# A fused sigmoid attention and MLP: from batch 2 on TensorE takes its work in the order of the program

## The chip, the cores and the metric

The kernel runs on one core of a Trainium2 chip. The metric is the device time of one execution in microseconds (us); lower is better. A core has five engines with a queue of instructions each: TensorE (PE, matmuls; its weight loads are listed apart as PEld), VectorE (DVE), ScalarE (ACT), GpSimd (POOL) and SyncE (SP, which here issues most transfers). An engine takes its queue in order, and an instruction waits there until semaphores tell that its operands are ready and its destination is free.

## The reference

```python
scores = scale * np.matmul(q, k.transpose(0, 1, 3, 2)) - np.log(S)
attn = 1.0 / (1.0 + np.exp(-scores))
x = np.matmul(attn, v)              # batch 8, heads 12, S = 448, D = 64; heads side by side: 3584 x 768
h = x @ w_in                        # 768 x 2048
g = np.where(h >= 1, h, np.where(h <= -1, 0.0, (h + 1) ** 2 / 4))
out = g @ w_out                     # 2048 x 768
```

All inputs and the output are float32.

## The kernel before

Numbers are split into a high and a low float16 part, and a product is three float16 matmuls (high x high, high x low, low x high). The first batches are prepared together with the weights; from batch 2 on the work of a batch is always the same (batch 7 has no attention beside it), and in it lies the change.

**Attention** works ahead: while batch b goes through the MLP, the attention of batch b + 1 is computed. Heads go in six pairs, and a pair is cut into four pieces of keys: three full ones (128 keys of both heads) and a middle one (64 keys of each head). `scores` writes a piece's scores to a PSUM tile `psc`, of which there are two: L416 and L411 with the whole array, L425 with two matmuls that use half of the array's rows each. L159 is one small matmul that sums a pair's magnitudes. `weigh` turns a piece into weights: sigmoid L457 (ScalarE, in place in `psc`), a cast to the high part L465 (ScalarE), the low part L466 (VectorE). `av` multiplies them with v, L498, in matmuls that use half of the array's columns and come in pairs. At a pair's end L507 copies the result out; L131 to L139, L359 and L360 (VectorE) make the scales of a later pair, and L344 (ScalarE) takes its magnitudes. GpSimd splits the raw q, k and v into parts (L378 to L380).

**The up product** (x @ w_in) goes in eight blocks i = 0 to 7. A block has seven products j = 0 to 6 of half size, written (i,j) here; each is a unit of nine matmuls of 224 columns (L688). The products are summed in quarters of two PSUM tiles `ph`: (i,0), (i,1) and (i,4) in the first, (i,2), (i,3), (i,5) and (i,6) in the second. Between them the kernel reads the tiles: L700 (ScalarE) and one L697 (VectorE) after (i,1), two L697 after (i,3), L706 (ScalarE) after (i,4), two L697 after (i,6). Then `bend` makes g: Relu L735 (ScalarE), L736 and L737 (VectorE), the cast L738 (ScalarE) and the low part L739 (VectorE), twice per block. The units' order is (0,0) to (0,3), and then, for each i, (i+1,0), (i+1,1), (i,4), (i,5), (i,6), (i+1,2), (i+1,3). L664 loads the weights of a block, three blocks ahead at most. **The down product** (g @ w_out) goes in 48 units of six matmuls of 448 columns (L758), eight to each of six output tiles `po`; L768 scales one, and it is stored. `ph` and `po` share three PSUM tiles.

**The order of the work.** For each batch the program has a list of units, 56 up and 48 down, and calls `step` between them at even distances until the next batch's attention is done, 12 unit places before the end. A step that does work writes the scores of two pieces and, behind them, `av` of the two pieces of the step before. There are 12 in a batch, called S0 to S11 here: S0 stands before (0,0), S1 to S7 lie in the up stage, some 7.7 units apart; even ones score a full and a middle piece, odd ones two full pieces.

What the program writes is not yet the order in which an engine takes it. A scheduler orders each engine's instructions by priority and a model of their times: where the next one of the program would not be ready in the model, it takes another. Only inside `manual_schedule` does an engine keep the order in which the program wrote its instructions. The loop over batches has this for TensorE, from batch `PM` on:

```python
            if b >= PM:
                order.enter_context(tc.manual_schedule(engines={mybir.EngineType.PE}))
```

With `PM = 9` and eight batches it is never entered.

Of the kernel before, what the change touches and what calls it, by code (L numbers as in the profile page):

```python
# [14 lines left out]
F32 = mybir.dt.float32  # L15
# [3 lines left out]
AF = mybir.ActivationFunctionType  # L19
ALU = mybir.AluOpType  # L20
# [3 lines left out]
P = 128  # L24
# [12 lines left out]
NA = 8  # L37
# [9 lines left out]
GPOOL = 1  # L47
POOL_FROM = 6
WI_SUM = 2
WO_SUM = 0  # L50
MAX_ACT = 47
L0 = 9
A0 = 19
# [2 lines left out]
SB = 2  # L56
# [4 lines left out]
MIXP = 0  # L61
CORN = 10
TP = 1

DW = 8
MIX0 = 8
MIX1 = 85
Q_PRIO = 72

PM = 9  # L70
WI_PRIO = 280
X_PRIO = 593

# [2 lines left out]
def sigmoid_attention_mlp(ctx: ExitStack, tc: tile.TileContext, first_qvk, qkv, w_in, w_out, out_t):  # L76
    nc = tc.nc
    NFULL, _, _, S = first_qvk.shape
    B = out_t.shape[1] // S
    NFC, _, DM = w_out.shape  # L80
# [6 lines left out]
    GROUPS = slice(0, NA), slice(NA, NFC)  # L87
# [7 lines left out]
    out_p = ctx.enter_context(tc.tile_pool(name="outp", bufs=2))  # L95
# [4 lines left out]
    ps_mo = ctx.enter_context(tc.tile_pool(name="ps_mo", bufs=3, space=PSUM))  # L100
# [24 lines left out]
    def scales(m, n, tag, pool=None, square=False, less=0):  # L125
# [24 lines left out]
        out=ident, in_=ident, pattern=[[-1, P]], compare_op=ALU.is_equal, fill=0.0, base=0, channel_multiplier=1  # L150
# [28 lines left out]
    class Weight:  # L179


        def __init__(self, dram, sb, name, spare):
            self.dram, self.sb, self.name, self.spare = dram.bitcast(I32), sb, name, spare
            self.words, self.at, self.loaded = {}, 0, 0
            self.scale, self.inv = [], []
            self.most = const.tile([P, 2, NFC], F32, name=name + "_most")
            nc.vector.memset(self.most, 0.0)
            mod = WI_SUM if name == "wi" else WO_SUM
            self.summed = [f for f in range(NFC) if mod and f % mod == 0 and f not in (NA - 1, NFC - 1)]

        def f32(self, f):
            return self.sb[:, f + 1].rearrange("p h n -> p (h n)").bitcast(F32)
# [16 lines left out]

        def convert(self):  # L210

            f = self.at - 2
            if 0 <= f < NFC:
                w = self.words.pop(f)
                if f in self.summed:

                    dump = wo.f32(-1) if self is wi else w[:, :DM].bitcast(F32)
                    nc.scalar.activation(dump, self.f32(f), AF.Abs, accum_out=self.most[:, 1, f : f + 1])
                if self is wo:
                    self.load(3 if f == 3 else 1)  # L220
            f = self.at
            if f < NFC:
                a = self.f32(f)
                nc.scalar.activation(a, self.words_of(f)[1].bitcast(F32), AF.Abs)
                if f in self.summed:
                    (nc.vector if f >= CLAMP else nc.gpsimd).tensor_scalar(
                        out=a, in0=a, scalar1=HIGH_MIN, scalar2=None, op0=ALU.max
                    )
            f = self.at - 1
            if 0 <= f < NFC:  # L230
# [395 lines left out]
    def mix(i):  # L626
# [87 lines left out]
    hold = {}  # L714
# [28 lines left out]
    def down(b, m, u, k):  # L743

        lo, hi = (0, NFC) if k is None else (GROUPS[k].start, GROUPS[k].stop)
        if u == 0:
            hold["po"] = ps_mo.tile([P, 512], F32, tag="mo", name="po")
            hold["o"] = out_p.tile([P, S], F32, tag="o", name="o")
            if m == 0:
                hold["od"] = down_sc[b, k]()  # L750
            if k == 1:
                nc.sync.dma_start(out=hold["o"], in_=part[m])
        po, o = hold["po"], hold["o"]

        pair = (u, u + NFC // 2) if b >= SB else (lo + 2 * u, lo + 2 * u + 1)
        for f in pair:
# [210 lines left out]
```

## Time and profile before

| | |
|---|---|
| time, median of 3 runs | 1190.35 us (1187.74 to 1190.66) |
| profiled execution: time, span | 1187.38 us, 1185.7 us |
| granted TensorE clock, mean | 0.991 |
| PE busy | 1144.9 us, 97% |
| DVE busy | 854.9 us, 72% |
| ACT busy | 697.6 us, 59% |
| POOL busy | 332.8 us, 28% |
| batch 3 on TensorE | from 529.17 us to 666.35 us |

An engine's share is an average over the span. A line of a group gives the source line, the engine, the operation, what it writes and reads, the count, then the busy time, the mean of one in ns, the idle time just before its instructions and what ended it. A line of a timeline gives the start, the length, the engine, the source line and the count of like instructions that follow each other.

### The profile page before, as it was taken

How to read it: one execution, taken by the hardware profiler on the slowest of the kernel's cores; microseconds unless marked ns; L12 is line 12 of the kernel's file. 1: busy time of each engine (PE TensorE's matmuls, PEld its weight loads, DVE VectorE, ACT ScalarE, POOL GpSimd, SP SyncE). 2: the span in 40 equal slices, each digit the busy share in tenths (PEclk: the TensorE clock that was granted, in tenths of full speed). 3: DMA queues.
4: the chain of work that ended last, by engine and by line, in shares of the span. 5: the costliest groups of instructions: out<-in, count | busy, mean ns of one | idle time of the engine just before them, and what ended most of it. 6: DMA issues, size and time to landing. Idle time of an engine off the chain costs nothing.

```text
span 1185.7 us, 20268 instructions
## 1 busy us (share of the span) xinstructions
PE 1144.9 (97%) x7662; PEld 669.3 (56%) x7662; DVE 854.9 (72%) x1828; ACT 697.6 (59%) x1158; POOL 332.8 (28%) x393
## 2 busy tenths in 40 slices
PE   5889899999999999999999999999999999999998
PEld 1224333444445776457754677557764577558954
DVE  6999999999956588457973689456884678736830
ACT  5886576665654577547864578455864476613510
POOL 3004410011323244234345235332532353310000
PEclk9899999999999999999999999999999999999999
DMA  9842354437542266224643065423552246302400
GB/s 367 322 153 76 118 161 152 134 119 257 182 148 72 95 217 210 76 72 142 238 163 102 30 236 208 135 64 128 204 211 64 65 147 220 126 24 87 163 16 32
DMA packets 58113, 170.01 MB, mean 143 GB/s; under 512 B 8608, under 2 KB 39840, under 8 KB 51872
## 3 DMA queue, kind: packets, MB, share of 16 engines
q1 hardware_dynamic: 56288, 159.29, 39.1%
q10 hardware_dynamic: 1728, 9.44, 2.2%
q8 instruction: 60, 0.98, 0.3%
q14 instruction: 37, 0.30, 0.1%
HBM read 126.94 MB, written 23.40 MB: 127 GB/s over the span
## 4 chain that ended last, share of the span: by engine, by line
PE 71%; DVE 17%; DMA 4%; ACT 3%; issue 2%; POOL 2%; SPq 0%; POOLq 0%; ACTq 0%; DVEq 0%
PE po L758 33%; PE ph L688 22%; PE pav L498 8%; PE psc L416 3%; PE psc L425 2%; PE ph L722 2%; DVE g L736 2%; PE psc L411 1%; DVE g L737 1%; DVE ghl L739 1%; DMA raw<-qkv 1%; DVE ahl L466 1%; DVE w_in_sb L244 1%; DVE mixa L632 1%; DVE w_out_sb L247 1%
## 5 line engine op out<-in xcount | busy, mean ns | idle before, releaser
L758 PE MATMUL po<-ghl,w_out_sb 128*128 128x448 f16 x2304 | 446.3, 353 | 1.5 <-DVE qkv_e L131 0.6
L758 PEld LDWEIGHTS <-w_out_sb 128*128 128x128 f16 x2304 | 221.7, 98 | 219.4 <-issue 15.9
L688 PE MATMUL ph<-w_in_sb 128*128 128x224 f16 x3024 | 307.7, 259 | 1.3 <-DVE g L737 0.9
L688 PEld LDWEIGHTS <-w_in_sb 128*128 128x128 f16 x3024 | 282.6, 98 | 30.1 <-issue 27.2
L466 DVE SCALAR_TENSOR_TENSOR ahl<-psc,ahl 128x896 f16<-128x896 f32 (+1 forms) x170 | 153.0, 900 | 105.7 <-ACT ahl L465 103.6
L378 POOL TENSOR_SCALAR raw<-raw,qkv_s 128x448 f32<-128x448 f32 (+1 forms) x93 | 71.0, 777 | 449.9 <-DVE qkv_i L139 346.3
L457 ACT ACTIVATE psc<-psc,nls,sqk 128x896 f32<-128x896 f32 (+1 forms) x136 | 129.5, 971 | 103.5 <-PE psc L425 86.6
L465 ACT ACTIVATE ahl<-psc 128x896 f16<-128x896 f32 (+1 forms) x170 | 126.9, 762 | 29.8 <-DVE ahl L466 28.6
L722 PE MATMUL ph<-xhl,w_in_sb 128*128 128x448 f16 x576 | 114.5, 356 | 4.7 <-DVE g L737 3.4
L344 ACT ACTIVATE dump<-raw 128x448 f16<-128x448 f32 (+1 forms) x105 | 61.9, 589 | 85.8 <-DMA raw<-qkv 84.5
L697 DVE TENSOR_TENSOR xhl<-ph,xhl 128x224 f32<-128x224 f32 x240 | 87.7, 383 | 25.3 <-PE ph L688 19.4
L738 ACT ACTIVATE ghl<-g 128x448 f16<-128x448 f32 x128 | 72.5, 573 | 44.2 <-DVE g L737 43.8
L498 PE MATMUL pav<-ahl,v 128*64 128x448 f16 x748 | 95.6, 360 | 0.0
L735 ACT ACTIVATE g<-xhl,hr,ihr 128x448 f32<-128x448 f32 x96 | 68.7, 752 | 41.9 <-DVE xhl L697 41.0
L722 PEld LDWEIGHTS <-w_in_sb 128*128 128x128 f16 x576 | 55.7, 99 | 63.6 <-issue 14.4
L736 DVE SCALAR_TENSOR_TENSOR g<-g,rk 128x448 f32<-128x448 f32 x112 | 81.4, 741 | 10.2 <-ACT g L735 10.0
L739 DVE TENSOR_TENSOR ghl<-g,ghl 128x448 f16<-128x448 f32 x128 | 85.0, 672 | 5.3 <-ACT ghl L738 4.8
L768 DVE TENSOR_SCALAR o<-po,od 128x448 f32<-128x448 f32 x48 | 32.5, 679 | 61.1 <-PE po L758 60.8
L380 POOL TENSOR_TENSOR hl<-raw,hl 128x448 f16<-128x448 f32 x62 | 71.1, 1167 | 0.0
L416 PE MATMUL psc<-qk 128*128 128x448 f16 x252 | 66.3, 354 | 2.0 <-ACT a L454 1.0
L737 DVE SCALAR_TENSOR_TENSOR g<-xhl,ihs,g 128x448 f32<-128x448 f32 x96 | 66.3, 708 | 0.3
L498 PEld LDWEIGHTS <-v 128*64 128x64 f16 x748 | 36.3, 109 | 37.9 <-issue 23.0
(167 smaller groups left out, 1198.5 us busy)
## 6 DMA issues: line engine op xcount, KB each, us to landing
w_in_sb<-blocks SPq DMA_DIRECT2D x48, 1344.0 KB, 6.1
raw<-qkv SPq DMA_DIRECT2D x34, 704.0 KB, 4.7
qk<-hl SPq DMA_DIRECT2D x320, 56.0 KB, 2.0
w_out_sb<-w_in SPq DMA_DIRECT2D x16, 768.0 KB, 8.5
out_t<-o SPq DMA_DIRECT2D x48, 224.0 KB, 1.9
blocks<-mixs SPq DMA_DIRECT2D x8, 768.0 KB, 3.5
w_out_sb<-w_out ACTq DMA_DIRECT2D x6, 768.0 KB, 4.1
raww<-w_out ACTq DMA_DIRECT2D x6, 768.0 KB, 5.7
```

The source lines that it names most:

```text
L416: nc.tensor.matmul(out, kq[:, j, 1, w], kq[:, j, 0, :], start=True, stop=False)
L457: nc.scalar.activation(a, a, AF.Sigmoid, bias=nls, scale=sqk)
L465: nc.scalar.activation(hi, x, AF.Copy, scale=ATT)
L466: nc.vector.scalar_tensor_tensor(out=lo, in0=x, scalar=ATT, in1=hi, op0=ALU.mult, op1=ALU.subtract)
L498: nc.tensor.matmul(pav[j * D : (j + 1) * D, :S], *terms[j][t], start=c == 0 and t == 0, stop=mid and t == len(terms[j]) - 1,)
L688: nc.tensor.matmul(out, w[:, wt, wh, c * P : (c + 1) * P], xc[:, xt, c, xh, :], start=j in (0, 2) and c + wh + xh == 0, stop=c == HC - 1 a ...
L697: add = lambda out, q, other: nc.vector.tensor_tensor(out=out, in0=quarter(q), in1=other, op=ALU.add)
L722: nc.tensor.matmul(ph[:, :S], w_in_sb[:, f, wh, c * P : (c + 1) * P], xhl[:, c, xh, :], start=c == 0 and wh + xh == 0, stop=c == NCC - 1 a ...
L736: nc.vector.scalar_tensor_tensor(out=g, in0=g, scalar=rt, in1=g, op0=ALU.min, op1=ALU.mult)
L737: nc.vector.scalar_tensor_tensor(out=g, in0=h, scalar=ihs, in1=g, op0=ALU.mult, op1=ALU.max)
L739: (nc.gpsimd if f % GPOOL else nc.vector).tensor_tensor(out=ghl[:, f, 1, :], in0=g, in1=hi, op=ALU.subtract)
L758: nc.tensor.matmul(po[:, :S], w_out_sb[:, f, wh, m * P : (m + 1) * P], ghl[:, f, gh, :], start=f == lo and wh + gh == 0, stop=f == hi - 1 ...
```

## The change

`PM` becomes 2: for batches 2 to 7 TensorE's instructions stand in the order of the program. Batches 0 and 1 are not touched, nor is any instruction added or removed. The scheduler still orders the other engines by its model, and since in the model TensorE now reaches its instructions at other times, the orders on VectorE, ScalarE and SyncE change with it. GpSimd's stays.

```diff
-PM = 9
+PM = 2
```

The rest of the diff leaves the work as it was: an accumulation in `convert` is written a few lines earlier in the same call, the tiles of `down` are kept under the name of their output tile, and new parameters (`SLAG`, `AM`, `MIXA`, `CUT`) stand at values that give the code of before.

```diff
-            hold["po"] = ps_mo.tile([P, 512], F32, tag="mo", name="po")
+            hold["po", m] = ps_mo.tile([P, 512], F32, tag="mo", name="po")
...
+        order = [(m, u) for m in range(NCC) for u in range(n // 2)]
+        if b >= SB:
+
+            first = [(m, u) for m in range(2) for u in range(CUT)] + [(m, u) for m in range(2) for u in range(CUT, n // 2)]
+            order[: n] = first
...
-    with tc.manual_schedule(engines={mybir.EngineType.SP}):
+    with tc.manual_schedule(engines={mybir.EngineType.SP} | ({mybir.EngineType.Activation} if AM else set())):
```

The added lines shift the numbers: a line of 131 to 139 in the kernel before is 3 higher in the changed one, one of 344 to 507 is 4 higher, one of 664 to 770 is 7 higher. The numbers in the names of tiles count tiles and differ a little between the two.

**TensorE, batch 3, step S5.** Before, after the first full piece's L416 (tile `psc_5969`) one of its two L425 is followed by products of block 4 and 5:

```order
L416 MATMUL psc_5969<-qk_5670 128x448
L425 LDWEIGHTS hl_5659
L425 MATMUL psc_5969<-hl_5659 128x448
L688 LDWEIGHTS w_in_sb_89
L688 MATMUL ph_5860<-w_in_sb_89 128x224
```

Now both pieces (`psc_5974`, `psc_5977`) are scored in one run, and `av` follows:

```order
L429 MATMUL psc_5974<-hl_5664 128x448
L429 LDWEIGHTS hl_5664
L429 MATMUL psc_5977<-hl_5664 128x448
L429 LDWEIGHTS hl_5664
L429 MATMUL psc_5977<-hl_5664 128x448
L502 LDWEIGHTS v_5359
L502 MATMUL pav_5830<-ahl_5821,v_5359 64x448
```

What moved is the products: they stand behind the whole step. Before, the step's second piece was scored five units later.

**VectorE, batch 3, from the additions after (1,6) to the two after (2,3)** (tiles `ph_5442` and `ph_5564` before, `ph_5447` and `ph_5569` now; the low parts L466 of S2's middle piece come in halves). Before:

```order
L697 TENSOR_TENSOR xhl_92<-ph_5442,xhl_92 128x224 x2
L466 SCALAR_TENSOR_TENSOR ahl_5523<-psc_5509,ahl_5523 64x448
L131 TENSOR_SCALAR qkv_e_5649<-psc_5509 128x3
L736 SCALAR_TENSOR_TENSOR g_5552<-g_5552,rk1_5145 128x448
L133 TENSOR_SCALAR qkv_e_5649<-qkv_e_5649 128x3
L697 TENSOR_TENSOR xhl_92<-ph_5564,xhl_92 128x224
L736 SCALAR_TENSOR_TENSOR g_5558<-g_5558,rk0_5135 128x448
L737 SCALAR_TENSOR_TENSOR g_5552<-xhl_92,ihs1_5149,g_5552 128x448
L135 TENSOR_SCALAR qkv_s_5652<-qkv_e_5649 128x3
L139 TENSOR_SCALAR qkv_i_5654<-qkv_e_5649 128x3
L697 TENSOR_TENSOR xhl_92<-ph_5564,xhl_92 128x224
```

Now:

```order
L704 TENSOR_TENSOR xhl_92<-ph_5447,xhl_92 128x224 x2
L470 SCALAR_TENSOR_TENSOR ahl_5524<-psc_5511,ahl_5524 128x896
L470 SCALAR_TENSOR_TENSOR ahl_5528<-psc_5514,ahl_5528 64x448
L743 SCALAR_TENSOR_TENSOR g_5557<-g_5557,rk1_5147 128x448
L704 TENSOR_TENSOR xhl_92<-ph_5569,xhl_92 128x224
L743 SCALAR_TENSOR_TENSOR g_5563<-g_5563,rk0_5137 128x448
L744 SCALAR_TENSOR_TENSOR g_5557<-xhl_92,ihs1_5151,g_5557 128x448
L470 SCALAR_TENSOR_TENSOR ahl_5528<-psc_5514,ahl_5528 64x448
L134 TENSOR_SCALAR qkv_e_5654<-psc_5514 128x3
L704 TENSOR_TENSOR xhl_92<-ph_5569,xhl_92 128x224
```

The low part of a whole piece and one more half piece have come between the two pairs of additions.

**ScalarE, batch 3, from the first sigmoid of S5 to the copy L706 after (5,4)** (tile `ph_5860` before, `ph_5865` now). Before:

```order
L457 ACTIVATE psc_5969<-psc_5969,nls_87,sqk_5656 128x2x448
L465 ACTIVATE ahl_5980<-psc_5969 128x896
L738 ACTIVATE ghl_93<-g_5795 128x448
L457 ACTIVATE psc_5972<-psc_5972,nls_87,sqk_5656 128x2x448
L735 ACTIVATE g_5911<-xhl_92,hr1_5153,ihr1_5151 128x448
L507 ACTIVATE x32_91<-pav_5825,sqk_5350 128x448
L735 ACTIVATE g_5917<-xhl_92,hr0_5143,ihr0_5141 128x448
L344 ACTIVATE dump_5965,m3_5964<-raw_5801 128x448
L465 ACTIVATE ahl_5984<-psc_5972 128x896
L706 ACTIVATE xhl_92<-ph_5860 128x224
```

Now, behind the two Relu of block 4 and one L348:

```order
L461 ACTIVATE psc_5974<-psc_5974,nls_87,sqk_5661 128x2x448
L461 ACTIVATE psc_5977<-psc_5977,nls_87,sqk_5661 128x2x448
L348 ACTIVATE dump_5970,m3_5969<-raw_5806 128x448
L745 ACTIVATE ghl_93<-g_5916 128x448
L511 ACTIVATE x32_91<-pav_5830,sqk_5355 128x448
L469 ACTIVATE ahl_5985<-psc_5974 128x896
L745 ACTIVATE ghl_93<-g_5922 128x448
L469 ACTIVATE ahl_5989<-psc_5977 128x896
L348 ACTIVATE dump_5970,m3_5969<-raw_5806 128x512
L707 ACTIVATE xhl_92<-ph_6017 128x224
L713 ACTIVATE xhl_92<-ph_5865 128x224
```

Both sigmoids now come first, and the copy that frees the product tile has moved behind both casts, two magnitudes and the copy of the next block.

More of the change, by code (lines that the diff above doesn't have):

```diff
@@ L49 @@
 WI_SUM = 2
-WO_SUM = 0
 MAX_ACT = 47
@@ L63 @@
 TP = 1
+SLAG = 2
+AM = 0
+MIXA = 0
+CUT = 8
 DW = 8
@@ L187, in __init__ @@
             nc.vector.memset(self.most, 0.0)
-            mod = WI_SUM if name == "wi" else WO_SUM
-            self.summed = [f for f in range(NFC) if mod and f % mod == 0 and f not in (NA - 1, NFC - 1)]
+            mod = WI_SUM if name == "wi" else 0
+            early = [f for g in GROUPS for f in range(g.start, g.stop - SLAG + 1)]
+            self.summed = [f for f in early if mod and f % mod == 0]
         def f32(self, f):
@@ L210, in convert @@
         def convert(self):
+            f = self.at - SLAG
+            if 0 <= f < NFC and f in self.summed:
+                nc.scalar.activation(wo.f32(-1), self.f32(f), AF.Abs, accum_out=self.most[:, 1, f : f + 1])
             f = self.at - 2
             if 0 <= f < NFC:
[L214 to L218, printed above, removed]
+                self.words.pop(f)
                 if self is wo:
@@ L654, in mix @@
             for h in range(2):
-                nc.vector.tensor_scalar(
-                    out=pv[:, h, t0 : t0 + n, :], in0=src[:, h], scalar1=to[k], scalar2=None, op0=ALU.mult
-                )
+                if MIXA:
+                    nc.scalar.activation(pv[:, h, t0 : t0 + n, :], src[:, h], AF.Copy, scale=to[k])
+                else:
+                    nc.vector.tensor_scalar(
+                        out=pv[:, h, t0 : t0 + n, :], in0=src[:, h], scalar1=to[k], scalar2=None, op0=ALU.mult
+                    )
         nc.sync.dma_start(out=blocks[i][:, : 3 * DM], in_=pl)
@@ L746, in down @@
         if u == 0:
-            hold["po"] = ps_mo.tile([P, 512], F32, tag="mo", name="po")
-            hold["o"] = out_p.tile([P, S], F32, tag="o", name="o")
+            hold["po", m] = ps_mo.tile([P, 512], F32, tag="mo", name="po")
+            hold["o", m] = out_p.tile([P, S], F32, tag="o", name="o")
             if m == 0:
@@ L751, in down @@
             if k == 1:
-                nc.sync.dma_start(out=hold["o"], in_=part[m])
-        po, o = hold["po"], hold["o"]
+                nc.sync.dma_start(out=hold["o", m], in_=part[m])
+        po, o = hold["po", m], hold["o", m]
         pair = (u, u + NFC // 2) if b >= SB else (lo + 2 * u, lo + 2 * u + 1)
@@ L788, in downs @@
         n = NFC if k is None else GROUPS[k].stop - GROUPS[k].start
-        return [lambda m=m, u=u: down(b, m, u, k) for m in range(NCC) for u in range(n // 2)]
+        order = [(m, u) for m in range(NCC) for u in range(n // 2)]
+        if b >= SB:
+            first = [(m, u) for m in range(2) for u in range(CUT)] + [(m, u) for m in range(2) for u in range(CUT, n // 2)]
+            order[: n] = first
+        return [lambda m=m, u=u: down(b, m, u, k) for m, u in order]
     def step(i):
```

## The prediction

> **What bounds the kernel now.** I read the page's busy shares and groups first, then the stretches by batch, then TensorE's timeline through one batch, then VectorE's and ScalarE's in the same batch.
>
> ```profile
> PE 1144.9 (97%) x7662; PEld 669.3 (56%) x7662; DVE 854.9 (72%) x1828; ACT 697.6 (59%) x1158; POOL 332.8 (28%) x393
> ...
> L758 PE MATMUL po<-ghl,w_out_sb 128*128 128x448 f16 x2304 | 446.3, 353 | 1.5 <-DVE qkv_e L131 0.6
> L688 PE MATMUL ph<-w_in_sb 128*128 128x224 f16 x3024 | 307.7, 259 | 1.3 <-DVE g L737 0.9
> ...
> L736 DVE SCALAR_TENSOR_TENSOR g<-g,rk 128x448 f32<-128x448 f32 x112 | 81.4, 741 | 10.2 <-ACT g L735 10.0
> ...
> w_in_sb<-blocks SPq DMA_DIRECT2D x48, 1344.0 KB, 6.1
> ```
>
> ```profile
> 545.00:605.00 60.00, 60.00 (x530) 45.51 (x528) 54.01 (x112) 47.58 (x88) 27.46 (x31) 1.00 0.63 220
> ```
>
> TensorE (PE) is the bound: 97% busy, and its two largest groups waited 1.5 and 1.3 us in all. So there is next to no idle time to win. But busy is not the same as streaming well, and the stretch from 545 to 605 (columns after the length: PE, weight loads, DVE, ACT, POOL) shows a second engine close behind: VectorE is busy 54.0 of 60.0 us in the up stage of batch 3.
>
> ```profile
> 529.17 0.54 PE L416 MATMUL psc<-qk 128*128 128x448 f16 x2
> ...
> 531.88 6.21 PE L688 MATMUL ph<-w_in_sb 128*128 128x224 f16 x63
> 537.92 0.54 PE L416 MATMUL psc<-qk 128*128 128x448 f16 x2
> 538.40 0.36 PE L425 MATMUL psc<-hl 64*128 64x448 f16 x2
> 538.69 0.55 PE L416 MATMUL psc<-qk 128*128 128x448 f16 x2
> ...
> 540.54 4.49 PE L688 MATMUL ph<-w_in_sb 128*128 128x224 f16 x45
> ...
> 572.38 0.36 PE L425 MATMUL psc<-hl 64*128 64x448 f16 x1
> 572.67 1.90 PE L688 MATMUL ph<-w_in_sb 128*128 128x224 f16 x18
> ...
> 599.71 3.76 PE L758 MATMUL po<-ghl,w_out_sb 128*128 128x448 f16 x19
> ...
> 603.31 1.89 PE L688 MATMUL ph<-w_in_sb 128*128 128x224 f16 x18
> ...
> 605.03 2.25 PE L758 MATMUL po<-ghl,w_out_sb 128*128 128x448 f16 x11
> ...
> 619.03 0.92 PE L416 MATMUL psc<-qk 128*128 128x448 f16 x4
> ...
> 621.43 8.12 PE L758 MATMUL po<-ghl,w_out_sb 128*128 128x448 f16 x42
> ...
> 629.39 0.54 PE L416 MATMUL psc<-qk 128*128 128x448 f16 x2
> ...
> 632.09 9.25 PE L758 MATMUL po<-ghl,w_out_sb 128*128 128x448 f16 x48
> ```
>
> Starts are what to read here, since ends are modelled: 63 L688 take 6.04 us (531.88 to 537.92), 0.096 each; 19 L758 take 3.60, 0.19 each. A pair of L425 halves takes 0.29 (538.40 to 538.69) and a lone half the same 0.29 (572.38 to 572.67): halves in one array run together, and each change between whole array, row halves and column halves adds about 0.1.
>
> **The gain.** In the down stage the order is already the program's, and a step stands whole there: 2.40 us with two full pieces (619.03 to 621.43), 2.70 with a middle piece (629.39 to 632.09). In the up stage the scheduler has cut the steps up. Batch 3's up stage runs from 529.17 to 605.03 and holds 3.60 us of L758 that program order puts later: 72.26 us of its own. Whole, it is S0 2.71, four steps of 2.40, three of 2.70 and 504 L688 at 6.04 per 63, 48.32: 68.7. So 3.5 us per batch of pure streaming goes, and the down stage, the same before and after, gives nothing.
>
> **The price.** Program order stops TensorE wherever the next matmul is not ready; the filler (L758 x19 at 599.71 above all) is what stood there before. I looked for such places by the waits that the order implies: a block's sixth product (i,5) overwrites the bank that both additions L697 after (i,3) read; a new PSUM tile for products waits for the last reader of the tile three back; a new score tile for L466 of the one two back. Prices are start to start, from these rows.
>
> ```profile
> 543.27 0.68 DVE L697 TENSOR_TENSOR xhl<-ph,xhl 128x224 f32<-128x224 f32 x2
> ...
> 543.86 1.08 DVE L466 SCALAR_TENSOR_TENSOR ahl<-psc,ahl 128x896 f16<-128x896 f32 x1
> 544.86 0.38 DVE L697 TENSOR_TENSOR xhl<-ph,xhl 128x224 f32<-128x224 f32 x1
> ...
> 545.16 1.27 DVE L736 SCALAR_TENSOR_TENSOR g<-g,rk 128x448 f32<-128x448 f32 x2
> ...
> 546.35 0.39 DVE L697 TENSOR_TENSOR xhl<-ph,xhl 128x224 f32<-128x224 f32 x1
> ...
> 546.65 1.27 DVE L737 SCALAR_TENSOR_TENSOR g<-xhl,ihs,g 128x448 f32<-128x448 f32 x2
> ...
> 574.40 0.63 DVE L466 SCALAR_TENSOR_TENSOR ahl<-psc,ahl 64x448 f16<-64x448 f32 x1
> 575.04 0.16 DVE L131 TENSOR_SCALAR qkv_e<-psc 128x3 f32<-128x3 f32 x1
> ```
>
> ```profile
> 538.12 0.36 ACT L706 ACTIVATE xhl<-ph 128x224 f32<-128x224 f32 x1 [0.51 <-PE ph L688]
> ...
> 538.80 2.06 ACT L457 ACTIVATE psc<-psc,nls,sqk 128x896 f32<-128x896 f32 x2 [0.32 <-PE psc L425]
> ...
> 540.78 0.92 ACT L465 ACTIVATE ahl<-psc 128x896 f16<-128x896 f32 x1
> 541.58 0.65 ACT L507 ACTIVATE x<-pav,sqk 128x448 f32<-128x448 f32 x1
> ...
> 542.10 0.93 ACT L465 ACTIVATE ahl<-psc 128x896 f16<-128x896 f32 x1
> ...
> 596.07 1.40 ACT L735 ACTIVATE g<-xhl,hr,ihr 128x448 f32<-128x448 f32 x2
> ...
> 597.38 0.56 ACT L344 ACTIVATE dump<-raw 128x448 f16<-128x448 f32 x1
> ...
> 600.79 0.57 ACT L738 ACTIVATE ghl<-g 128x448 f16<-128x448 f32 x1
> 601.26 0.62 ACT L344 ACTIVATE dump<-raw 128x512 f16<-128x512 f32 x1
> ...
> 601.87 0.35 ACT L706 ACTIVATE xhl<-ph 128x224 f32<-128x224 f32 x1
> 602.11 0.57 ACT L738 ACTIVATE ghl<-g 128x448 f16<-128x448 f32 x1
> ```
>
> A product reaches ScalarE 0.20 after its slot (537.92 to 538.12). DVE: two L697 0.59, one 0.30, L466 1.00 or 0.64 (half), L736 and L737 0.60. ACT: two L735 1.31, L344 0.56 or 0.61, two L457 1.98, L465 0.80, L507 0.52, L738 0.47, L700/L706 0.24.
>
> *A, (1,5).* Its second addition ended at 546.74. In the new order S1's first score tile is done 0.38 later (two more L416 ahead), so 547.12. TensorE, with S1 at 2.40 instead of 2.62 (537.92 to 540.54), reaches (1,5) after seven units, at 546.36. Wait 0.7.
>
> *B, (2,5).* After (1,6) VectorE's queue is the one shown with the change: 0.20 + 0.59 + 1.00 + 0.64 + 0.60 + 0.30 + 0.60 + 0.60 + 0.64 + 0.16 + 0.39 = 5.7. TensorE asks after five units, 45 L688, 4.3. Wait 1.4. Behind it stand (2,6) and S3, for whose results the Relu of block 2 and the sigmoids wait.
>
> *C, S4's middle piece.* It needs L466 of S3's second tile. From (2,6): 0.2, about 0.5 that VectorE is behind after B, 0.45 for the addition and its hand-over, then ScalarE's queue 1.31 + 0.56 + 1.98 + 0.52 + 0.56 + 0.47 + 0.80 + 0.47 + 0.93 = 7.6, and 0.35 + 1.08 to the end of L466: 10.2. TensorE asks after S3, seven units and two L416: 2.40 + 6.04 + 0.38 = 8.8. Wait 1.4.
>
> *D, (6,2).* It needs L706 of block 5, which now stands last in ScalarE's queue shown with the change. From (4,6): 0.9 to the first Relu, then 1.31 + 0.56 + 1.98 + 0.56 + 0.47 + 0.52 + 0.80 + 0.47 + 0.80 + 0.61 + 0.24 + 0.36 = 8.7: 9.6. TensorE asks after 0.86 + 2.40 + 5.18 = 8.4. Wait 1.2.
>
> Together 4.7 us per batch; the ends are 0, if every chain is ready in time, and 7.5, if two more places like C open (the rivals). I take the sum, since each place is priced by rows of its own engine. The durations are those of quiet stretches: L736 is 0.64 here and 0.74 in its group's mean, so I add 0.3 for the longer ones: 5.0, against 3.5 gained. Batches 2 to 6 do this: 5 x 1.5 = +7.5. The waits that were there, 2.8 in the two groups, are of another order; I take half as gone, -1.4. Batch 7, which has no attention left, and the first two batches, whose order stands, count nothing. SP's queue changes in one thing per batch: a weight load moves ahead of six qk loads, and at 6.1 us to landing, with more than nine units and a step (over 10 us) between issue and use, I cost that at nothing; if the queue held it 4 us longer, it would show on (i,0). POOL's order is the same.
>
> Sum: +6.1 on the profiled execution's 1187.38, which is 1193.5; the median of the runs lies 3.0 above that execution, so **1196**.
>
> The Trainium skill (TensorE: Matmul & The Clock Gate, Why this matters for your kernels) says that an idle gap beyond about 3 us puts TensorE back to half its clock. By that rule the waits above, at most 1.4, change nothing; the stretch 545 to 605 has its clock at 1.00, but also no gap, so no row here tests it.
>
> **Rivals.**
> *The gain stays (faster).* The four waits are differences of numbers near 6 to 10 us: half a microsecond less in each chain, because VectorE enters the stage earlier or ScalarE's queue is not full, leaves 2.5 of 5.0. For it: VectorE and ScalarE were idle 6.0 and 12.4 us in the 60, partly waiting on TensorE. Against: VectorE's 54.0 us of work there must now go beside 60 - 3.6 - 3.5 = 52.9 us of TensorE's. Time: 1190.35 - 5 x 1.0 - 1.4 = 1184; with no wait left at all 1190.35 - 17.5 - 2.8 = 1170. It decides at 3.0 us of waits per batch.
> *Gain and waits cancel.* Waits of 3.0 to 4.5 per batch: 1187 to 1194.
> *Waits run into each other.* A late L466 holds the next scores, these the next sigmoids: two more waits of the size of C in S5 and S7 add 2.8 per batch, 1196 + 14 = 1210. Against: between S4 and S5 and between S6 and S7 more units stand than between S3 and S4.
> *A wait passes 3 us.* By rows, a half-speed stretch of 18 L688 would cost 1.7 more after it, 5 x (3 + 1.7) = 24: 1214. This is the outcome that the clock rule above would add.
> That the change does nothing is excluded: the orders differ.
>
> **How the numbers follow.** About 0.3% (3.6 us) is what a measurement of this kernel tells from no change. Forecast, slower by 4 to 16 us: 0.45. Gain stays: 0.27. Cancel: 0.21. Waits run into each other 0.05, clock 0.02. So faster 0.27, same 0.21, slower 0.52. The forecast's own range is 1194 to 1206; to hold 8 in 10 the range takes in the faster case down to half its spread, 1178, and goes up to 1207.
>
> **What would show it.** Right: in the up stages every step is one run of L416, L425 and L498 on TensorE, S1 about 2.40; TensorE's idle time grows to some 25 us, put down to L697 (places A and B), L466 (C) and L706 (D), in batches 2 to 6 alike; the down stages keep their 61 us. Wrong: idle time under 15 us (then the chains are shorter than summed), waits ended by DMA, or a down stage that changes, which I hold for fixed.

## The result, and the profile after

| | before | after |
|---|---|---|
| time, median | 1189.05 us (4 runs, 1187.06 to 1190.66) | 1204.38 us (4 runs, 1201.26 to 1208.53) |
| ratio, 95% interval | | 1.0115 (1.0090 to 1.0141) |
| profiled execution: time, span | 1187.38 us, 1185.7 us | 1203.64 us, 1201.9 us |
| granted TensorE clock, mean | 0.991 | 0.986 |

Slower by 15.3 us; the forecast was 6 us slower than the median of then. One execution of e4 and one of e10 ran at a lower granted clock (0.75 and 0.94; 1456.48 and 1216.30 us), and the medians given below leave them out. The page of the changed kernel, busy shares and costliest groups:

```profile
PE 1134.1 (94%) x7662; PEld 672.8 (56%) x7662; DVE 867.9 (72%) x1828; ACT 696.8 (58%) x1158; POOL 337.0 (28%) x393
...
L765 PE MATMUL po<-ghl,w_out_sb 128*128 128x448 f16 x2304 | 444.7, 353 | 1.0 <-DVE qkv_e L134 0.6
...
L695 PE MATMUL ph<-w_in_sb 128*128 128x224 f16 x3024 | 301.2, 260 | 20.9 <-DVE xhl L704 15.6
...
L743 DVE SCALAR_TENSOR_TENSOR g<-g,rk 128x448 f32<-128x448 f32 x112 | 89.6, 815 | 10.9 <-ACT g L742 10.2
```

TensorE is busy for 10.8 us less, and the span is 16.2 us longer: idle time grew by 27. The products (L695) wait 20.9 us where they waited 1.3. The waits of TensorE in the whole execution (us in total, times, longest):

```profile
PE ph L695 <- DVE xhl L704: 15.6, 12, 3.7
...
PE psc L415 <- DVE ahl L470: 5.8, 6, 1.1
PE ph L695 <- ACT xhl L713: 5.2, 4, 1.3
...
PE psc L420 <- DVE ahl L470: 1.1, 5, 0.2
```

TensorE's timeline through the up stage of batch 3; the idle time ahead of a row and what ended it stand in brackets:

```profile
534.31 0.54 PE L420 MATMUL psc<-qk 128*128 128x448 f16 x2
...
543.06 0.92 PE L420 MATMUL psc<-qk 128*128 128x448 f16 x4
...
545.46 6.27 PE L695 MATMUL ph<-w_in_sb 128*128 128x224 f16 x63
552.29 1.02 PE L695 MATMUL ph<-w_in_sb 128*128 128x224 f16 x9 [0.56 <-DVE xhl L704]
...
555.85 5.35 PE L695 MATMUL ph<-w_in_sb 128*128 128x224 f16 x54
562.78 1.89 PE L695 MATMUL ph<-w_in_sb 128*128 128x224 f16 x18 [1.57 <-DVE xhl L704]
...
566.90 6.21 PE L695 MATMUL ph<-w_in_sb 128*128 128x224 f16 x63
573.33 0.55 PE L420 MATMUL psc<-qk 128*128 128x448 f16 x2 [0.22 <-DVE ahl L470]
574.95 0.73 PE L415 MATMUL psc<-hl,w_in_sb 128*128 128x448 f16 x3 [1.07 <-DVE ahl L470]
...
586.59 5.35 PE L695 MATMUL ph<-w_in_sb 128*128 128x224 f16 x54
593.25 1.88 PE L695 MATMUL ph<-w_in_sb 128*128 128x224 f16 x18 [1.31 <-ACT xhl L713]
...
608.72 5.84 PE L765 MATMUL po<-ghl,w_out_sb 128*128 128x448 f16 x30
...
673.65 0.54 PE L420 MATMUL psc<-qk 128*128 128x448 f16 x2
```

Counted in units of nine from the step ahead of them, the four stops are (1,5), (2,5), S4 and (6,2): the places A to D, in order. Now the same two executions by batch, from one (0,0) on TensorE's timeline to the next:

| stretch | before | after | difference | forecast |
|---|---|---|---|---|
| start to (0,0) of batch 2 | 394.45 | 397.80 | +3.35 | 0 |
| batches 2, 3, 4, 5 | 137.43, 137.18, 137.26, 137.93 | 139.21, 139.35, 139.20, 139.20 | +1.78, +2.17, +1.94, +1.27 | 4 x 1.5 |
| batch 6 | 133.68 | 139.12 | +5.44 | 1.5 |
| batch 7 to the end | 107.78 | 108.03 | +0.25 | 0 |

Up to the second score tile of S1 in batch 2 every engine has the same instructions in the same order in both kernels, so the first row is no effect of the order. In the profiles of this study whose text is the same up to there (e4's, at its lower clock, apart), (0,0) of batch 2 came between 393.6 and 400.2 us, with either order.

Batch 6 stands out. TensorE, VectorE and then the clock there (TensorE and VectorE as timelines, the clock as a window, its value the one before the last two columns):

```profile
995.03 4.49 PE L695 MATMUL ph<-w_in_sb 128*128 128x224 f16 x45
1003.23 4.15 PE L695 MATMUL ph<-w_in_sb 128*128 128x224 f16 x27 [3.71 <-DVE xhl L704]
```

```profile
993.15 0.38 DVE L704 TENSOR_TENSOR xhl<-ph,xhl 128x224 f32<-128x224 f32 x1
996.14 1.68 DVE L350 TENSOR_REDUCE m<-raw 128x2 f32<-128x896 f32 x2 [2.62 <-DMA raw<-qkv]
997.74 1.27 DVE L743 SCALAR_TENSOR_TENSOR g<-g,rk 128x448 f32<-128x448 f32 x2
...
1002.79 0.38 DVE L704 TENSOR_TENSOR xhl<-ph,xhl 128x224 f32<-128x224 f32 x1
```

```profile
1003.20:1008.00 4.80, 4.77 (x30) 3.74 (x30) 3.92 (x13) 1.41 (x2) 2.51 (x4) 0.64 0.32 89
```

The last pair's magnitudes are taken on VectorE (L350), not on ScalarE like the others. VectorE stood 2.62 us before them for their load, with the Relu's work and the additions L704 after (4,3) queued behind; TensorE stood 3.71 us at (4,5), and then ran at clock 0.64. The 27 L695 after the wait take 3.94 us instead of 2.59 (27 x 0.096). Before, the same instruction stood for the same load (the instructions of L346, what their engine waited for):

```profile
L346 DVE TENSOR_REDUCE m<-raw x2: 676/881/1086, 985.5 to 986.5; 128x2 f32<-128x896 f32 x1, 128x1 f32<-128x512 f32 x1
...
  DMA raw<-qkv: 2.7, 1
```

But there the scheduler had put other matmuls on TensorE, which waited 0.4 us in that stretch.

### The profile page after: what moved, and what is told of

It is laid out like the page before. It is cut to its first block, busy times and chain, and to the rows that moved or that the text cites. A ratio compares the mean times of both kernels' runs of the same rounds, so it can differ in the third digit from the quotient of the medians.

```text
span 1201.9 us, 20263 instructions
## 1 busy us (share of the span) xinstructions
PE 1134.1 (94%) x7662; PEld 672.8 (56%) x7662; DVE 867.9 (72%) x1828; ACT 696.8 (58%) x1158; POOL 337.0 (28%) x393
## 4 chain that ended last, share of the span: by engine, by line
PE 60%; DVE 27%; ACT 6%; DMA 3%; issue 3%; POOL 1%; SPq 0%; POOLq 0%; DVEq 0%; ACTq 0%
PE po L765 33%; PE ph L695 13%; PE pav L502 6%; DVE ahl L470 4%; DVE g L743 3%; PE psc L420 3%; DVE g L744 2%; DVE ghl L746 2%; DVE xhl L704 2%; PE psc L429 2%; PE psc L415 2%; ACT psc L461 1%; PE ph L729 1%; DVE mixa L636 1%; DMA blocks<-mixs 1%
## 5 line engine op out<-in xcount | busy, mean ns | idle before, releaser
L765 PE MATMUL po<-ghl,w_out_sb 128*128 128x448 f16 x2304 | 444.7, 353 | 1.0 <-DVE qkv_e L134 0.6
L765 PEld LDWEIGHTS <-w_out_sb 128*128 128x128 f16 x2304 | 221.8, 98 | 219.5 <-issue 14.3
L695 PE MATMUL ph<-w_in_sb 128*128 128x224 f16 x3024 | 301.2, 260 | 20.9 <-DVE xhl L704 15.6
L695 PEld LDWEIGHTS <-w_in_sb 128*128 128x128 f16 x3024 | 287.4, 98 | 38.8 <-issue 37.8
L470 DVE SCALAR_TENSOR_TENSOR ahl<-psc,ahl 128x896 f16<-128x896 f32 (+1 forms) x170 | 152.8, 899 | 122.1 <-ACT ahl L469 120.2
L348 ACT ACTIVATE dump<-raw 128x448 f16<-128x448 f32 (+1 forms) x105 | 61.9, 590 | 77.0 <-DMA raw<-qkv 75.6
L704 DVE TENSOR_TENSOR xhl<-ph,xhl 128x224 f32<-128x224 f32 x240 | 87.1, 382 | 22.6 <-PE ph L695 18.4
L743 DVE SCALAR_TENSOR_TENSOR g<-g,rk 128x448 f32<-128x448 f32 x112 | 89.6, 815 | 10.9 <-ACT g L742 10.2
L729 PEld LDWEIGHTS <-w_in_sb 128*128 128x128 f16 x576 | 55.6, 98 | 64.4 <-issue 15.2
L746 DVE TENSOR_TENSOR ghl<-g,ghl 128x448 f16<-128x448 f32 x128 | 86.2, 676 | 4.7 <-ACT ghl L745 3.8
L502 PE MATMUL pav<-ahl,v 128*64 128x448 f16 x748 | 84.5, 357 | 0.0
L744 DVE SCALAR_TENSOR_TENSOR g<-xhl,ihs,g 128x448 f32<-128x448 f32 x96 | 70.3, 754 | 0.0
L384 POOL TENSOR_TENSOR hl<-raw,hl 128x448 f16<-128x448 f32 x62 | 68.8, 1132 | 0.0
L420 PE MATMUL psc<-qk 128*128 128x448 f16 x252 | 63.3, 355 | 3.6 <-DVE ahl L470 1.1
L411 PE MATMUL psc<-ghl 64*128 64x448 f32 (+1 forms) x128 | 38.1, 681 | 18.6 <-ACT a L458 14.2
```

The costliest lines, as they stand in the source:

```text
L420: nc.tensor.matmul(out, kq[:, j, 1, w], kq[:, j, 0, :], start=True, stop=False)
L470: nc.vector.scalar_tensor_tensor(out=lo, in0=x, scalar=ATT, in1=hi, op0=ALU.mult, op1=ALU.subtract)
L502: nc.tensor.matmul(pav[j * D : (j + 1) * D, :S], *terms[j][t], start=c == 0 and t == 0, stop=mid and t == len(terms[j]) - 1,)
L695: nc.tensor.matmul(out, w[:, wt, wh, c * P : (c + 1) * P], xc[:, xt, c, xh, :], start=j in (0, 2) and c + wh + xh == 0, stop=c == HC - 1 a ...
L704: add = lambda out, q, other: nc.vector.tensor_tensor(out=out, in0=quarter(q), in1=other, op=ALU.add)
L729: nc.tensor.matmul(ph[:, :S], w_in_sb[:, f, wh, c * P : (c + 1) * P], xhl[:, c, xh, :], start=c == 0 and wh + xh == 0, stop=c == NCC - 1 a ...
```

## The experiments

Theory: program order saves some 3.5 us per batch in streaming, and its price is the waits at A to D, plus the load in batch 6. Rivals: the loss lies outside batches 2 to 6; whole steps save nothing; the waits are not tied to their places, since VectorE and ScalarE are simply full. Ratios are against the kernel before, with their 95% intervals.

**e1, batch 7 alone.**

```diff
-PM = 2
+PM = 7
```

> Program order on TensorE in batch 7 alone, which has no attention beside its products. Theory (the loss sits in the up stages of batches 2 to 6): within 2 us of the kernel before, so 1187 to 1191, with one wait of about 1.3 us in batch 7 (as at 1141.87 in the changed kernel). Rival (the 3.4 us by which the changed kernel was already late at the start of batch 2, where its order is the old one, or something in batch 7, belongs to the change): 1192 or more.

1189.84 us, ratio 0.9999 (0.9983 to 1.0015). Batch 7 waits 1.26 us at its last (7,5) and the time is unchanged. The first rival falls.

**e2, batches 6 and 7.**

```diff
-PM = 2
+PM = 6
```

> Program order on TensorE in batches 6 and 7 alone. Theory: batch 6 has a price of its own, since VectorE stands 2.6 us before L350 for a load of raw q, k and v, and in program order TensorE then has nothing else to take: a wait of 3.7 us and a slow stretch after it, so 133.7 us from (0,0) to (0,0) become 139.1 and the time is 1189 + 5.4 = 1194 to 1195. Rival (each batch of program order costs the same, a fifth of the 15): 1192, with no wait above 2 us.

1198.50 us, ratio 1.0074 (1.0051 to 1.0097). TensorE in batch 6:

```profile
998.03 5.20 PE L695 MATMUL ph<-w_in_sb 128*128 128x224 f16 x27 [3.59 <-DVE xhl L704]
```

The wait is there, and the 27 products behind it take 4.99 us. Batch 6 is 140.2 us, 6.5 more than before. So batch 6 has a price of its own, larger than both expectations; of the 8.6 us in the medians, 2 are not accounted for.

**e3, the last magnitudes on ScalarE.**

```diff
-MAX_ACT = 47
+MAX_ACT = 48
```

> The changed kernel (program order from batch 2), with the last pair's magnitudes on ScalarE like all others instead of L350 on VectorE. Theory: VectorE no longer stands before the load, so the 3.7 us wait at (5,5) of batch 6 goes, the wait at (6,2) of 1.3 us that the other batches have comes in its place, and the granted clock stays at 1.00 there: batch 6 falls from 139.1 to 136.5 us and the time from 1204.4 to about 1201.5. Rival (the load is what TensorE waits for, whichever engine reads it): ScalarE stands before it instead, and the time stays at 1204.

1198.22 us, ratio 1.0066 (1.0045 to 1.0087). (The wait that the expectation places at (5,5) is the one at (4,5).) Batch 6 on TensorE:

```profile
994.36 7.07 PE L695 MATMUL ph<-w_in_sb 128*128 128x224 f16 x72
...
1003.68 5.35 PE L695 MATMUL ph<-w_in_sb 128*128 128x224 f16 x54
1010.33 1.89 PE L695 MATMUL ph<-w_in_sb 128*128 128x224 f16 x18 [1.30 <-ACT xhl L713]
```

No wait at (4,5), no slow stretch, and D as in the other batches: batch 6 takes 135.0 us in place of 139.1. Batches 2 to 5 are unchanged at 139.2. The gain in the medians, 6.2 us, is more than batch 6's 4.1.

**e7, the same edit in the old order.**

```diff
-PM = 2
+PM = 9
-MAX_ACT = 47
+MAX_ACT = 48
```

> The order of before, with the last pair's magnitudes on ScalarE instead of L350 on VectorE: the control for the same edit under program order, which went from 1204.4 to 1198.2. Theory (in the old order the scheduler's filler covers the 2.7 us for which VectorE stands before the load, all but 0.4): no change, 1188.5 to 1190.5. Rival (the edit saves time by itself): 1185 or less.

1189.19 us, ratio 0.9980 (0.9964 to 0.9996): a gain, if any, of 0.2%. In the profile batch 6 takes 132.9 us instead of 133.7. What cost batch 6 4.1 us in program order cost it 0.8 in the scheduler's.

**e6, the steps one unit earlier.** The places move, the amount of work does not:

```diff
-... (at - first) < share[min(u + 1, last)] * NPIECE:
+... (at - first) < share[min(u + 0, last)] * NPIECE:
```

> The changed kernel with each step written one unit earlier among the products. Theory (the price is the four places, each a difference between two chains of 6 to 10 us, so it moves with the places): (2,5) now comes after the low part in VectorE's queue and S4 stands elsewhere, so B and C go; what stays is about 0.5 at (1,5), 1.1 at (4,2) and 1.1 at (6,2), 2.8 us in a batch in place of 4.7, and a batch takes 137 us in place of 139.2: 1194 to 1197. Rival (VectorE is full in the up stage, so that the waits only change place): 4.5 to 5 us of waits as before, 1202 to 1206.

1191.55 us, ratio 0.9996 (0.9981 to 1.0012). The stops in batch 3:

```profile
551.83 1.89 PE L695 MATMUL ph<-w_in_sb 128*128 128x224 f16 x18 [0.29 <-DVE xhl L704]
...
572.15 1.02 PE L695 MATMUL ph<-w_in_sb 128*128 128x224 f16 x9 [1.24 <-ACT xhl L713]
...
591.21 2.75 PE L695 MATMUL ph<-w_in_sb 128*128 128x224 f16 x27 [1.69 <-ACT xhl L713]
```

B and C are gone and A is halved; D, the last, is 1.69, and a stop of 1.24 at (4,2) is new. The expectation had these places, with 1.1 for each of the last two. 3.2 us of idle time remain of 4.7. A batch takes 137.4 us, as in the old order, and in batch 6 no stop is longer than 1.04 us. The time lies below the range of the theory, 1194 to 1197. One unit in the place of the steps is worth all that the change had cost (ratio 0.9996 for 1.0115); the waits belong to places. That VectorE is full whatever the place does not fit.

**e4 and e5, program order within a step alone.** The gain without the price, if they can be had apart:

```diff
-PM = 2
+PM = 9
...
-                    step(at)
+                    with ExitStack() as whole:
+                        if b >= 2:
+                            whole.enter_context(tc.manual_schedule(engines={mybir.EngineType.PE}))
+                        step(at)
```

> The kernel before, except that TensorE keeps the program's order within a step alone: the products are free to move between steps and into them. The up stage of batch 3 then changes its array layout 41 times, as often as the changed kernel, instead of 63 times, and no half matmul stands alone. Theory (whole steps save some 3.5 us per batch, and the price of the changed kernel is the waits of the products): most of the gain without most of the price, 1182 to 1187, with less than 3 us of waits in an up stage. If no wait were left, 1172. Rival (whole steps save nothing, and the saving of the changed kernel is only the idle time subtracted): 1189.

1201.26 us, ratio 1.0091 (1.0069 to 1.0114): a miss. (The expectation's 41 and 63 changes of layout fit batch 3 as a whole, where the traces have 42 and 64 from one (0,0) to the next; the up stage alone has 28 in the changed kernel and 49 in the one before.) For its profile the kernel was run again.

> The same kernel as in the run before it with program order within a step alone, for a profile at full clock; the time is known to be near 1201. Theory 1 (the freed products meet waits that an estimate of them left out, some of them long enough to cost clock): TensorE's waits in the up stages of batches 2 to 6 sum to more than 4 us per batch, and a batch takes about 139.5 us. Theory 2 (a step in one piece is not cheaper in streaming): waits below 2 us per batch, the batch still 139 us or more. Theory 3 (the loss is ahead of batch 2): batches of 136 us.

1200.24 us, ratio 1.0065 (1.0045 to 1.0085). The profiled execution, 1193.26 us, was the shortest of eight, so what follows explains less than the median lost. TensorE in batch 3, and the clock behind the first two stops:

```profile
566.59 0.55 PE L420 MATMUL psc<-qk 128*128 128x448 f16 x2 [0.74 <-DVE ahl L470]
568.69 4.60 PE L695 MATMUL ph<-w_in_sb 128*128 128x224 f16 x29 [1.55 <-DVE xhl L704]
...
644.55 0.54 PE L420 MATMUL psc<-qk 128*128 128x448 f16 x2 [0.76 <-issue]
```

```profile
570.00:575.00 5.00, 5.00 (x36) 3.57 (x36) 3.60 (x8) 0.90 (x2) 0.00 (x0) 0.72 0.95 389
```

Batches 2 to 5 take 138.0, 139.2, 140.3 and 137.3 us; their waits sum to 2.8 to 4.3 us, some in the down stage, and three stretches lose clock, one each in batches 3, 4 and 6. The third theory falls (137 to 140, not 136), the second too (waits above 2), and of the first the waits are right in kind but a little short of 4 us. Which of the orders that moved with it makes the down stage wait was not traced further.

**e8, the waits placed away.** Here the program is written for the waits: (i,4) ahead of (i+1,0), `av` apart from its scores, and the edit of e3.

```diff
-MAX_ACT = 47
+MAX_ACT = 48
+SCORES_AT = [0, 5, 16, 23, 31, 38, 46, 53, 61, 69, 76, 84]
+AV_AT = [0, 8, 21, 26, 33, 41, 46, 53, 61, 69, 76, 84]
...
+            order += [(i, 4)]
             if i + 1 < n:
                 order += [(i + 1, 0), (i + 1, 1)]
-            order += [(i, 4), (i, 5), (i, 6)]
+            order += [(i, 5), (i, 6)]
...
+                for k in range(12):
+                    for which, place in enumerate((SCORES_AT, AV_AT)):
+                        if SB <= b < B - 1 and place[k] == u:
+                            step(first + 2 * k, which)
```

> Program order on TensorE from batch 2, but of another program: in each block (i,4) stands ahead of (i+1,0), so that L713 has two units more before (i+1,2) needs it; the scores of a step and its av are written apart, av of S1 to S5 two to five units behind their scores, where TensorE waited; and the last pair's magnitudes are on ScalarE. Going through the queues of a batch with the durations of the traces leaves no wait in batches 2 to 6. Theory (program order saves 3.5 us per batch in streaming, and the price is only the waits): batches of 133.6 us in place of 139.2 (and of 137.2 before), so 1171 to 1177, faster than both. Rival (VectorE and ScalarE are too full in the up stage to keep up without the idle time): waits come back elsewhere, 1185 or more.

1196.81 us, ratio 1.0048 (1.0028 to 1.0068), in the range of the rival; the profiled execution, 1192.07 us, was the shortest of twelve. A, B and D are gone. C is not: S4's middle piece still waits, 0.92 us where it and the piece before it waited 1.29. Two new places stop TensorE, the last block's (7,5) and the start of the down stage. All stops of batch 3:

```profile
568.58 0.73 PE L417 MATMUL psc<-hl,w_in_sb 128*128 128x448 f16 x3 [0.92 <-DVE mb L161]
...
599.65 1.89 PE L697 MATMUL ph<-w_in_sb 128*128 128x224 f16 x18 [0.84 <-DVE xhl L706]
...
613.41 0.35 PE L767 MATMUL po<-ghl,w_out_sb 128*128 128x448 f16 x1 [1.22 <-ACT ghl L747]
614.07 6.78 PE L767 MATMUL po<-ghl,w_out_sb 128*128 128x448 f16 x35 [0.31 <-DVE ghl L748]
```

Ahead of the first of them, VectorE and GpSimd (line numbers are two higher than in the changed kernel):

```profile
556.01 0.63 DVE L748 TENSOR_TENSOR ghl<-g,ghl 128x448 f16<-128x448 f32 x1
...
563.63 1.31 DVE L748 TENSOR_TENSOR ghl<-g,ghl 128x448 f16<-128x448 f32 x1
564.86 1.08 DVE L472 SCALAR_TENSOR_TENSOR ahl<-psc,ahl 128x896 f16<-128x896 f32 x1
565.86 1.57 DVE L748 TENSOR_TENSOR ghl<-g,ghl 128x448 f16<-128x448 f32 x1
```

```profile
563.42 2.41 POOL L386 TENSOR_TENSOR hl<-raw,hl 128x448 f16<-128x448 f32 x2
565.80 1.15 POOL L386 TENSOR_TENSOR v<-raw,v 128x512 f16<-128x512 f32 x1
```

The low part of g, 0.63 us alone at 556.01, takes 1.31 and 1.57 while GpSimd splits q, k and v; L472, which has one operand in PSUM, keeps its 1.08. The two stretched ones alone add 1.6 us ahead of the L472 for which S4's middle piece waits, and its stop is 0.92. The walk through the queues had used the durations of quiet stretches.

**e9, the same text in the scheduler's order.**

```diff
-PM = 2
+PM = 9
```

> The text of the run e8_waits_placed with the scheduler's order on TensorE throughout (PM = 9). Theory (the scheduler cuts the steps up again, so the streaming saved is lost, but it covers its waits): batches of 136 to 137 us, 1183 to 1189, slower than with program order. Rival (the gain of e8_waits_placed comes from the text alone, not from program order): the same time as that run.

1195.64 us, ratio 1.0046 (1.0025 to 1.0066), against 1.0048 for e8: the two orders cost the same on this text. The rival's time came, but not for its reason: e8 had no gain that the text could have brought. Batch 3's up stage is cut up again (49 changes of array layout, as in the kernel before; 31 in e8), and its down stage stops once for 3.07 us.

**e10, batch 7 left to the scheduler.**

```diff
-            if b >= PM:
+            if PM <= b < B - 1:
```

> As e8_waits_placed, but program order ends with batch 6, and batch 7, which has no steps, is left to the scheduler. Theory (the wait of 1.3 us that program order brings to batch 7 is all that it does there): 1.5 us less than e8_waits_placed. Rival (batch 7 is bound by its products whatever the order, as in the run with program order there alone): the same time.

1194.45 us, ratio 1.0037 (1.0019 to 1.0055). From (0,0) of batch 7 to the end it is 106.6 us instead of 108.1, as the theory expected; the intervals of the two kernels overlap and do not separate them.

**e11, e8 with less on GpSimd from pair 30 on.** The low parts of q, k and v of these pairs are left out.

```diff
+            if p >= LIGHT:
+                nc.gpsimd.tensor_scalar(out=hi, in0=rt, scalar1=s[:, t : t + 1], scalar2=1.0, op0=ALU.mult, op1=ALU.mult)
+                nc.gpsimd.memset(dst[:, 1, :], 0.0)
+                continue
```

> The run e8_waits_placed with less work on GpSimd from pair 30 on: one instruction to the high part and a fill with zeros, in place of three instructions, for each of q, k and v; the low parts of these pairs are left out. Pairs from 30 are prepared beside batches 4 to 6, so batches 2 and 3 of the same execution are the comparison. Theory (the waits that came back in e8_waits_placed are VectorE's instructions with two operands in SBUF, L745, L746 and L748, which take 0.94 to 1.57 us beside GpSimd instead of 0.62 to 0.68, and a raw load that is issued late because GpSimd holds the buffer): batches 2 and 3 stay at 138.3 us, batches 4 and 5 fall to 134 to 135, batch 6 from 132.3 to about 130. Rival (VectorE and ScalarE are full in the up stage whatever GpSimd does): 138 us in all.

1184.86 us, ratio 0.9956 (0.9940 to 0.9973). Batches 2 and 3 take 138.4 us, 4 and 5 134.8 and 135.0, 6 takes 130.6. VectorE's low part of g in batch 3 and then in batch 5 (count, busy time, mean):

```profile
L753 DVE TENSOR_TENSOR ghl<-g,ghl 128x448 f16<-128x448 f32 x16 | 13.3, 836 | 3.5 <-ACT ghl L752 3.4
```

```profile
L753 DVE TENSOR_TENSOR ghl<-g,ghl 128x448 f16<-128x448 f32 x16 | 9.8, 622 | 1.2 <-ACT ghl L752 0.9
```

Same order on TensorE, same execution: with GpSimd lighter the stops of 3.3 us become 0.43 in batch 4 and 0.43 + 0.28 in batch 5, and batch 4 is 2.5 us shorter than in the old order. That is the streaming gain without the price, shown on a kernel that leaves work out. How much of the 3.4 us between the batches is VectorE's stretch and how much the earlier load was not separated.

**e12, placed again.** As e10, with places chosen with the stretched durations.

```diff
-SCORES_AT = [0, 5, 16, 23, 31, 38, 46, 53, 61, 69, 76, 84]
-AV_AT = [0, 8, 21, 26, 33, 41, 46, 53, 61, 69, 76, 84]
+SCORES_AT = [0, 5, 16, 23, 32, 38, 46, 53, 61, 69, 76, 84]
+AV_AT = [0, 8, 19, 26, 34, 38, 46, 53, 61, 69, 76, 84]
```

> As e10_placed_b2_to_6 (program order in batches 2 to 6, scores and av written apart), with places chosen after going through the queues again with VectorE's and GpSimd's instructions stretched where they lie beside each other: S4 one unit later, av of S2, S4 and S5 two to three units earlier or directly behind the scores, av of S4 one later. Theory: waits of about 1.2 us in a batch in place of 3.3, batches of 135 to 136.5 us, 1180 to 1187, faster than both kernels. Rival (each shift of places trades one wait for another of its size): 1190 to 1195, as e10_placed_b2_to_6.

1179.49 us, ratio 0.9921 (0.9900 to 0.9942): faster than the kernel before, and by some 25 us than the changed one. The page's busy shares and the only stops of batch 3:

```profile
PE 1130.0 (96%) x7662; PEld 670.1 (57%) x7662; DVE 869.2 (74%) x1826; ACT 694.5 (59%) x1164; POOL 334.9 (28%) x393
```

```profile
575.88 0.54 PE L422 MATMUL psc<-qk 128*128 128x448 f16 x2 [0.57 <-DVE qkv_e L136]
...
584.11 1.88 PE L697 MATMUL ph<-w_in_sb 128*128 128x224 f16 x18 [0.86 <-ACT xhl L715]
```

Batches 2 to 5 take 135.8 to 135.9 us, batch 6 131.7. TensorE is busy for 14.9 us less than before and the idle time is 47.4 us, 6.6 more. Its text was not run in the scheduler's order, so how much of the gain on this text is program order's was not shown, and e12 differs from the changed kernel in the magnitudes, in the place of (i,4) and in batch 7 as well as in the places of the steps.

## Why the prediction was right in sign and short in size

**The gain.** Right. The up stage of batch 3 goes from 534.31 to 608.72, 74.41 us. The stops, start to start (the slot where TensorE asks, 0.096 per product after the last start, to the next start), are 0.79, 1.75, 0.39 + 1.24 and 1.48, together 5.65. That leaves 68.76, against 68.7 forecast: 3.5 saved. S1 takes 2.40 (543.06 to 545.46).

**The four places.** Right in place, order, engine and cause, in all of batches 2 to 5; each a little short. (B's chain, from the end of (1,6) at 556.71 to the end of the second addition at 562.72, took 6.0 us where 5.7 had been summed.)

| place | forecast | start to start | idle in the trace |
|---|---|---|---|
| A, (1,5) | 0.7 | 0.79 | 0.56 |
| B, (2,5) | 1.4 | 1.75 | 1.57 |
| C, S4 | 1.4 | 1.63 | 0.22 + 1.07 |
| D, (6,2) | 1.2 | 1.48 | 1.31 |

With the 0.3 for longer rows 5.0 were forecast and 5.65 measured, +0.65 per batch. The idle column is smaller than start to start by 0.17 to 0.23 a stop, since the modelled end of the last matmul reaches past its slot; the forecast was in slots and is to be held against slots.

**Batches 2 to 6 alike.** This step failed. Batches 2 to 5 came to +7.2, with 6.0 forecast; batch 6 to +5.4, with 1.5. Its wait of 3.71 in D's stead (+2.4) and the slow stretch behind it (1.35 on the 27 products, 0.3 on the scores) make 4.1 of it, and e3 takes out 4.1. The prediction looked for chains from TensorE's results back to TensorE, and not for an instruction in VectorE's queue that waits for a load; the 2.7 us were to be seen in the trace of before, and "waits ended by DMA" was named only as a sign that it would be wrong. The idle time was named by the instruction that came last, L704; the load stood two steps behind it.

**The clock.** The rival with a chance of 0.02 came true in one batch of five. The Trainium skill's rule of about 3 us (TensorE: Matmul & The Clock Gate, Why this matters for your kernels), which the prediction quoted, agrees with the trace there: after 3.71 us the clock was 0.64 on average over 4.80 us. Shorter stops cost clock too (last section).

**The other terms.** The old waits: L695 lost the 1.3 us that L688 had and L765 has 1.0 for 1.5, so 1.8 are gone, 1.4 forecast. Batch 7: 0 forecast, 0.25 in the trace, no change in e1. Down stage: 61.32 us before (605.03 to 666.35) and, less the 3.60 of products of the down stage that moved into it, 61.33 after (608.72 to 673.65). "Some 25 us" of idle time, put down to L704, L470 and L713: 27.7 us in the four rows of waits. SP's queue: no stop of TensorE was ended by a weight load.

**The sum.** 7.5 - 1.4 = 6.1 for batches 2 to 6, measured 12.6. The missing 6.5 are batch 6 (3.9) and the undersized stops (2.6 over four batches). The rest of the profiled difference, 3.4, stands ahead of batch 2 and is not the change's. The interval of the ratio puts the cost at 10.7 to 16.8 us; the 12.9 from batch 2 on lie inside. That 1204.38 still lies in the forecast's own range, 1194 to 1206, is owed to the width of that range: 7.3 of the 16.2 us, the 3.9 and the 3.4, come from what the prediction did not have.

**The other rivals.** "The gain stays" has a slip: half a microsecond less in each of four chains leaves 3.0 of 5.0, not 2.5, and its time is then 1186, not 1184. "Waits run into each other" did not happen: no stop in S5 or S7. "The gain stays" needed less than 3.0 us of waits per batch; e6, with 3.2 idle, came out even, and e12, with 1.4, faster, so the point of decision was about right.

## What to carry to other kernels

Before an order is fixed by hand, walk each queue that feeds the engine, and price every stop from slot to slot; there is a saving only where the stops together cost less than the streaming gains. Look above all for single instructions in the feeding queues that wait for a transfer, in any one batch: a scheduler's filler hides them, a fixed order passes them on whole. If the stops are few and always in the same places, move the program by a unit instead of giving up the order: here that was worth 12 us (e6), and the two halves of a step placed apart, with the other edits of e12, 25. The durations for such a walk must be those of the stretch in question: beside GpSimd they were up to 2.6 times as long (next section).

## What the hardware showed that I had not expected

**VectorE beside GpSimd.** In the traces of all kernels here but e4's, from batch 2 on, L743, L744 and L746 (two operands in SBUF) take 0.61 to 0.69 us when GpSimd is idle and up to 1.60 when it works throughout; L470 (1.08), L704 (0.38) and L512 (0.61), with at most one operand in SBUF, never change. GpSimd can pay too: L384 on 128x448 takes 1.03 to 1.05 alone and up to 1.69 where a part of it lies beside such an instruction. The Trainium skill (SBUF — State Buffer, Who interferes with whom) states just this: two SBUF inputs contend with a GpSimd instruction that reads SBUF, one does not. e8 and e11 agree.

**Clock after shorter stops.** In e9 the down stages of batches 2, 3, 4 and 5 stop once each, for 2.18, 3.07, 2.52 and 2.13 us. The clock just behind the stops of batches 3, 4 and 5:

```profile
615.00:620.00 5.00, 3.50 (x11) 1.45 (x11) 2.50 (x4) 4.28 (x8) 0.00 (x0) 0.66 0.02 6
757.00:762.00 5.00, 4.65 (x25) 2.44 (x25) 2.37 (x4) 3.62 (x6) 0.00 (x0) 1.00 0.00 0
896.00:901.00 5.00, 4.74 (x17) 2.10 (x17) 2.34 (x4) 3.58 (x6) 0.00 (x0) 0.66 0.00 0
```

It fell after 3.07 and after 2.13, not after 2.52 and not after 2.18; in e5 it fell in batch 3 after 0.74 and 1.55 with two matmuls between, and not in batches 2 and 4 with the same pair. So the length alone does not decide, and 3 us is not a safe bound.

The traces show what goes with it. In each profile the stretches at half clock last 3.41 us or a multiple of it (the one that the end cuts off apart), and all start on one grid of 3.41 us that runs through the execution. Each profile but e4's was cut into windows on its own grid, and from 300 us on 3375 of them ran at full clock. In ten TensorE was busy, as the profile counts it, for 41% or less, and the next window ran at half clock every time. In six it was busy for 45 to 49%, and half clock followed once. In all others it was busy for more, and half clock never followed.

| stop | busy share of the windows it lies in | clock of the window after |
|---|---|---|
| e9, batch 2: 2.18 | 0.46 (472.89 to 476.30), 0.90 | 1.00 |
| e9, batch 3: 3.07 | 0.18 (612.83 to 616.25), 0.93 | 0.50 after the first |
| e9, batch 4: 2.52 | 0.60 (752.78 to 756.20), 0.66 | 1.00 |
| e9, batch 5: 2.13 | 0.41 (892.73 to 896.14), 0.96 | 0.50 after the first |
| e5, batch 3: 0.74 + 1.55 | 0.36 (565.96 to 569.38) | 0.50 |
| e5, batch 4: 0.73 + 1.56 | 0.54 (705.91 to 709.32) | 1.00 |
| changed kernel, batch 6: 3.71 | 0.58, 0.33 (1000.96 to 1004.37) | 0.50 after the second |

Here a stop of 2.1 us that fell into one window cost clock, and one of 2.5 that two windows shared cost none. The phase of the grid against the first instruction differs from profile to profile (0.32 to 3.12 us), so the program does not set where a stop lies on it.
